# Sums of halves of hT for the second FFN matmul's seven products: two pieces of six inner blocks instead of three of 6, 4 and 2

## The chip, the cores and the metric

The kernel runs on one core of a Trainium2 chip. The core has five engines, each with an instruction queue of its own that is worked off in order: TensorE (PE, with PEld for its weight loads), VectorE (DVE), ScalarE (ACT), GpSimd (POOL) and SyncE (SP), which issues DMAs; POOL issues DMAs too. [...] The metric is device time in microseconds of one execution, and the number quoted is the median of several. Lower is better.

## The reference

Inputs are q, k, v of shape (8, 12, 448, 64) and two FFN weights, 768 x 3072 and 3072 x 768. What is computed:

```python
scores = scale * np.matmul(q, k.transpose(0, 1, 3, 2))
attn = np.maximum(scores, 0.0) ** 2 / S
x = np.matmul(attn, v)            # then heads side by side: (8, 448, 768)
X = np.fft.fft(np.fft.fft(x, axis=1), axis=2)
u = x + np.real(X)
un = (u - mean(u)) / np.sqrt(var(u) + 1e-06)      # over the 768 channels
out = u + np.maximum(un @ w_ch1, 0.0) @ w_ch2
```

## The kernel before

**Stages.** Attention runs by batch and group of four heads: scores on PE (L954), square of the positive part on ACT and DVE (L967, L981, L984), values on PE (L822 and six L827 in a block). The Fourier mix of a batch is a matmul with cosine and sine tables (L1432), a second small one over rows (L1240), and a normalisation on DVE, ACT and POOL. The normalised rows go through DRAM and come back transposed as unT. The FFN then works on groups of token columns: group 0 has 384 tokens, group 1 has 512, group 2 has 384, and the nine groups behind them 256 each. Its hidden layer hT is kept as 24 blocks of 128 hidden channels.

**First FFN matmul.** L1930 makes hT block by block into PSUM (tiles psF), and a relu, on ACT (L1917) or DVE (L1915), puts it into hT. Groups 8 to 11 do it otherwise, two groups at a time ("joints"; there are two): their first matmul is L1762, with sums of weight quarters made by DVE (L1661) and sums of unT (L1705); ACT takes copies out (L1777, L1806) and DVE adds them up (L1782). Of such two groups the first has its hidden layer in hT and the second in tiles hB.

**Second FFN matmul.** Groups 0 to 2 do some of their 128-token halves as plain products (L1958, L1985). Every other pair of halves, L and R, is done by an object of class `Pair` (L2018 on) with seven products instead of eight. There are eleven pairs: one for each of groups 1 to 7, and two in each joint. With the 24 blocks taken as twelve inner blocks of index 0 (even) and twelve of index 1 (odd), four sums are made on DVE:

- s1 = R0 + R1 (L2047), s2 = s1 - L0 (L2049) and R0 := L0 - R0 in place (L2051), all in `early`;
- L1 := L1 - s2 in place (L2059), in `late`.

The products are L2071, twelve matmuls of 128 x 384 each. Chain A does L0 with W11, then s2 with T2, then s1 with T1, then the new L1 with W22, all into one PSUM bank; chain B does the old L1 with W21, and then, into another, the new R0 with T3 and R1 with T4. T1 to T4 are sums of weights, made by DVE at L1526. Behind most products an addition (L1623, DVE) adds the bank to the output tile o, which comes from DRAM with the residual; the next product of the same chain goes on in the same bank, so it has to wait for that addition. While one chain waits, the other chain's product can run.

**Pieces.** The sums are made in pieces of inner blocks, `CH` (L1486). A piece waits for the relus of its own blocks alone. s1 and s2 have a home for the first six inner blocks (tiles s1, s2) and another for the last six (the upper part of the hT tile, `upper`, which is free from group 1's end on). The second group of a joint cuts the pieces once more where hB changes tile, at inner blocks 6, 8 and 10.

**Order.** All instructions of all engines are placed by a scheduler in the kernel (`Streams.run`, L72): each piece of work is a generator that says which engine it needs, how long it will take there by a formula (for these sums `dve2`, elements/1920 + 0.14 us), and what it waits for. The scheduler always takes the one that can start first by its own clock. So a different length or number of instructions at one place moves what comes behind on every engine. A few matmuls more or less of the FFN are put between attention blocks as they become due.

Of the kernel before, what the change touches and what calls it, by code (L numbers as in the profile page):

```python
# [149 lines left out]
def need(eng, dur, deps=(), bufs=(), ok=None):  # L150
    return eng, dur, list(deps), list(bufs), ok
# [18 lines left out]
def dve2(n):  # L170
    return Port(n / 1920 + 0.14)
# [6 lines left out]
def kernel(  # L178
# [34 lines left out]
    KP = 12  # L213
# [1269 lines left out]
    DH = D // 2  # L1483
    WHOLES = [[0, 1, 2], [2, 3], [2]] + [[]] * (NGR - 3)
    PAIRS = [[], [0]] + [[0]] * (NGR - 2)
    CH = [(0, 6), (6, 10), (10, KP)]  # L1486

    def upper(at, count, width):

        flat = hid[0].rearrange("p j n -> p (j n)")  # L1490
        return flat[:, at:at + count * width].rearrange("p (i n) -> p i n", n=width)

    hid, made = [], []
# [239 lines left out]
    def joint(number):  # L1733
# [112 lines left out]
        for i in range(KP):  # L1846
            sch.add(main(i), (5 + 0.1 * i, 5 + 0.1 * i))
        skip = lambda us: None
        plain = [(k, i0, i1) for k, (i0, i1) in enumerate(CH)]
        cut = [(k, max(i0, c0), min(i1, c1)) for k, (i0, i1) in enumerate(CH) for c0, c1, _ in hb  # L1850
               if max(i0, c0) < min(i1, c1)]
# [22 lines left out]
    def ffn(b):  # L1874
# [49 lines left out]
        for j in range(0, JC, JN):  # L1924
# [9 lines left out]
            if j == JC // 2:  # L1934
                ffn_begun[b].t = e
                at = lambda k, i0, i1, cols: h[:, 2 * i0 + k:2 * i1:2, cols]
                pairs = [Pair(b, c, at, ht, add, advance, [(k, *ch) for k, ch in enumerate(CH)], BF) for c in PAIRS[b]]
                for p in pairs:
# [79 lines left out]
    class Pair:  # L2018
# [14 lines left out]
        def early(self):  # L2033

            at, L, R_ = self.at, self.L, self.R
            if not made:
                yield need("DVE", 0.0, [un_left])
                a1 = work.tile([128, 6, 128], BF16, name="s1", tag="un2", bufs=1)
                a2 = work.tile([128, 6, 128], BF16, name="s2", tag="un3", bufs=1)
                at_ = JC * 256 + KP * DH  # L2040
                for a, m in ((a1, upper(at_, 6, 128)), (a2, upper(at_ + 6 * 128, 6, 128))):
                    made.append([a, m[:, 0:4], m[:, 4:6]])
            for x, (k, i0, i1) in enumerate(self.pieces):
                s1, s2 = (self.sums(n, i0, i1) for n in range(2))
                d = dve2((i1 - i0) * 128)
                yield need("DVE", d, self.ht[2 * i0:2 * i1] + self.waits + ([upper_free] if k else []))
                nc.vector.tensor_tensor(s1, at(0, i0, i1, R_), at(1, i0, i1, R_), op=ALU.add)  # L2047
                yield need("DVE", d)
                nc.vector.tensor_tensor(s2, s1, at(0, i0, i1, L), op=ALU.subtract)  # L2049
                e = yield need("DVE", d)  # L2050
                nc.vector.tensor_tensor(at(0, i0, i1, R_), at(0, i0, i1, L), at(0, i0, i1, R_), op=ALU.subtract)  # L2051
                self.r12[x].t = e + LATENCY["DVE"]
# [10 lines left out]
        def sums(self, n, i0, i1):  # L2063

            k = [c0 <= i0 < c1 for c0, c1 in CH].index(True)
            return made[n][k][:, i0 - CH[k][0]:i1 - CH[k][0]]

# [147 lines left out]
```

## Time and profile before

| | us |
|---|---|
| three runs | 569.48, 569.09, 566.94 |
| median | 569.09 |
| span of the profiled execution | 566.4 |
| PE busy | 556.5 |
| DVE busy | 436.2 |
| ACT busy | 318.2 |
| POOL busy | 195.9 |

The span runs from the first to the last instruction of one execution. Its own time is not listed apart from the span: the span lies 0.5 us below the fastest of the three runs and 2.7 us below their median. Busy time is the time in which an engine had an instruction in work; matmuls are pipelined, so for PE the distance from one matmul's start to the next one's says more than its busy time.

### The profile page before, as it was taken

What the parts mean: (1) busy time and instruction counts of PE and PEld (TensorE: products, weight loads), DVE (VectorE), ACT (ScalarE), POOL (GpSimd) and SP (SyncE); (2) the same over time, 40 slices, a digit from 0 to 9 for tenths busy, and PEclk for the clock granted to TensorE, in tenths of its full rate; (3) what the DMA queues carried; (4) which work ended last, traced back from release to release, by engine and by line L of the source; (5) the groups of instructions that cost most, each with busy time, mean ns of one, the idle gap of its engine ahead of it and who ended that gap; (6) DMA issues with size and microseconds to landing.
All of it is one profiled execution on the core that took longest, in us unless ns stands there. A gap on an engine that the chain in (4) does not pass through costs nothing.

```text
span 566.4 us, 11147 instructions
## 1 busy us (share of the span) xinstructions
PE 556.5 (98%) x4171; PEld 350.1 (62%) x4171; DVE 436.2 (77%) x1016; ACT 318.2 (56%) x536; POOL 195.9 (35%) x281
## 2 busy tenths in 40 slices
PE   7999999999999999999999999999999999999997
PEld 4376556544465455556756757767678688668864
DVE  7976564987789978887997896888899957644762
ACT  5978762676745686585786637638515154015400
POOL 8966225523346234462545545222015000000000
PEclk9999999999999999999999999999999999999999
DMA  9999999979959988899899979956425421231012
GB/s 110 180 209 230 215 215 165 217 144 134 181 96 210 215 117 179 164 187 184 174 163 196 198 121 198 164 123 154 115 65 174 124 75 29 71 127 56 1 57 83
DMA packets 152688, 82.41 MB, mean 146 GB/s; under 512 B 118076, under 2 KB 147900, under 8 KB 152636
## 3 DMA queue, kind: packets, MB, share of 16 engines
q0 software_dynamic: 57056, 33.63, 43.0%
q1 hardware_dynamic: 95580, 48.09, 38.1%
q8 instruction: 32, 0.52, 0.4%
q14 instruction: 20, 0.16, 0.1%
HBM read 62.91 MB, written 26.25 MB: 157 GB/s over the span
## 4 chain that ended last, share of the span: by engine, by line
PE 86%; DMA 5%; DVE 4%; ACT 2%; POOL 1%; issue 1%; DVEq 0%; POOLq 0%; ACTq 0%
PE psF L1930 25%; PE psF L2071 20%; PE psS L1762 8%; PE psS L954 7%; PE psS L2071 5%; DMA kn<-in_k_dram 5%; PE psF L827 5%; PE psF L1985 4%; PE psS L1432 2%; PE psF L1762 2%; PE psF L1958 2%; PE psF L822 1%; PE psF L623 1%; DVE sq L984 1%; PE psS L827 1%
## 5 line engine op out<-in xcount | busy, mean ns | idle before, releaser
L1930 PE MATMUL psF<-unT,w 128*128 128x256 bf16 (+2 forms) x1152 | 165.3, 299 | 0.0
L967 ACT ACTIVATE sq<-psS 128x896 bf16<-128x896 f32 x168 | 144.1, 919 | 31.7 <-PE psS L954 31.2
L1930 PEld LDWEIGHTS <-w 128*128 128x128 bf16 x1152 | 110.9, 98 | 49.6 <-issue 5.2
L984 DVE TENSOR_TENSOR sq<-sq 128x896 bf16<-128x896 bf16 x144 | 88.9, 634 | 13.3 <-ACT sq L967 12.5
L2071 PEld LDWEIGHTS <-hT 128*128 128x128 bf16 x648 | 62.5, 98 | 44.1 <-issue 4.8
L1917 ACT ACTIVATE hT<-psF 128x512 bf16<-128x512 f32 (+2 forms) x121 | 59.6, 508 | 41.1 <-PE psF L1930 40.3
L1623 DVE TENSOR_TENSOR o<-psF,o 128x384 f32<-128x384 f32 (+1 forms) x78 | 42.6, 547 | 24.3 <-PE psF L2071 20.8
L2071 PE MATMUL psF<-w,hT 128*128 128x384 bf16 x336 | 59.7, 326 | 0.6 <-DVE o L1623 0.6
L954 PE MATMUL psS<-qkT 64*128 64x448 bf16 (+1 forms) x336 | 51.5, 354 | 1.0 <-DVE qkT L630 0.8
L1777 ACT COPY copies<-psS 128x256 f32<-128x256 f32 x57 | 19.9, 374 | 53.0 <-PE psS L1762 48.1
L689 DVE TENSOR_SCALAR xT<-psF 128x224 bf16<-128x224 f32 x60 | 20.6, 384 | 26.1 <-PE psF L827 26.1
L1275 POOL TENSOR_TENSOR u<-tp,xn 112x385 f32<-112x385 f32 (+2 forms) x14 | 14.5, 1037 | 72.6 <-DVE tp L1255 48.6
L476 POOL DMA_DIRECT2D qn<-in_q_dram x21 | 15.7, 747 | 57.7 <-DVE qkr L583 50.3
L827 PE MATMUL psF<-sq,vn 128*64 128x448 bf16 x246 | 33.0, 362 | 0.0
L954 PEld LDWEIGHTS <-qkT 64*128 64x128 bf16 (+1 forms) x336 | 12.9, 94 | 32.3 <-issue 26.4
L1762 PEld LDWEIGHTS <-w 128*128 128x128 bf16 x288 | 28.2, 98 | 4.7 <-issue 1.1
L451 POOL DMA_DIRECT2D kn<-in_k_dram x42 | 25.9, 626 | 10.3 <-DMA w<-in_moe_w_ch_dram 6.0
L1284 DVE BATCH_NORM_STATS2 stats<-u 112x6 f32<-112x384 f32 (+2 forms) x56 | 28.7, 543 | 0.8 <-POOL u L1275 0.6
L451 POOL DMA_DIRECT2D vn<-in_v_dram x42 | 26.1, 638 | 6.2 <-DMA w<-in_moe_w_ch_dram 5.4
L476 POOL DMA_DIRECT2D vn<-in_v_dram x24 | 18.9, 789 | 25.5 <-PE psS L954 25.4
L1303 ACT ACTIVATE un<-u,small 112x768 bf16<-112x768 f32 (+2 forms) x22 | 22.0, 1023 | 9.5 <-DVE small L1290 8.4
L1782 DVE CUSTOM_DVE_ANT_0 hT<-psS,copies 128x256 bf16<-128x256 f32 x37 | 15.0, 421 | 14.1 <-PE psS L1762 6.2
(238 smaller groups left out, 946.9 us busy)
## 6 DMA issues: line engine op xcount, KB each, us to landing
out_dram<-o SPq DMA_DIRECT2D x55, 192.0 KB, 2.3
qn<-in_q_dram POOLq DMA_DIRECT2D x21, 224.0 KB, 5.1
vn<-in_v_dram POOLq DMA_DIRECT2D x24, 192.0 KB, 5.6
w<-in_moe_w_ch_dram POOLq DMA_DIRECT2D x12, 384.0 KB, 11.8
w<-in_moe_w_ch_dram POOLq DMA_DIRECT2D x4, 1152.0 KB, 23.4
kn<-in_k_dram POOLq DMA_DIRECT2D x21, 192.0 KB, 5.9
utop<-u SPq DMA_DIRECT2D x12, 336.0 KB, 2.9
o<-utop SPq DMA_DIRECT2D x16, 192.0 KB, 3.7
```

What stands on the lines that cost most here:

```text
L451: nc.gpsimd.dma_start(out=t[par * Dh:(par + 1) * Dh, par::2], in_=at)
L476: nc.gpsimd.dma_start(out=to, in_=src[b, hs, 0:rows].rearrange("h (p j) d -> p h (j d)", j=j))
L827: nc.tensor.matmul(av[h * Dh:(h + 1) * Dh, 0:S], lhsT=vn_home[:, at:at + Dh], rhs=sq[:, h, :], start=start, stop=stop, skip_group_check=True)
L954: nc.tensor.matmul(sc[:, h, 0:S].rearrange("k (c q) -> k c q", c=4), lhsT=flat[ps, k0:k0 + KB], rhs=qT[ps, pair], start=True, stop=True)
L967: nc.scalar.activation(r, sc[:, :, 0:S], AF.Relu)
L984: nc.vector.tensor_tensor(r, r, r, op=ALU.mult)
L1284: nc.vector.bn_stats(stats[:n, hf, :], u[:n, hf * (D // 2):(hf + 1) * (D // 2)])
L1623: nc.vector.tensor_tensor(o[:, cols], pc[:, cols], o[:, cols], op=ALU.add)
L1762: nc.tensor.matmul(ps[:, 0:N], lhsT=lhs, rhs=rhs[:, m], start=(start and m == 0), stop=(stop and m == 2), skip_group_check=True)
L1917: nc.scalar.activation(hs, ps, AF.Relu)
L1930: nc.tensor.matmul(ph[:, i * N:(i + 1) * N], lhsT=w1_sb[m][hf][:, (jj + i) * 128:(jj + i + 1) * 128], rhs=unT[:, m, 0:N], start=(m == 0), ...
L2071: nc.tensor.matmul(pc[:, cols], lhsT=lhs[i], rhs=rhs[i][:, cols], start=(start and i == 0), stop=(i == KP - 1), skip_group_check=True)
```

## The change

The table of pieces gets two entries instead of three, and the list of homes for s1 and s2 follows.

```diff
     WHOLES = [[0, 1, 2], [2, 3], [2]] + [[]] * (NGR - 3)
     PAIRS = [[], [0]] + [[0]] * (NGR - 2)
-    CH = [(0, 6), (6, 10), (10, KP)]
+    CH = [(0, 6), (6, KP)]
...
                 for a, m in ((a1, upper(at_, 6, 128)), (a2, upper(at_ + 6 * 128, 6, 128))):
-                    made.append([a, m[:, 0:4], m[:, 4:6]])
+                    made.append([a, m])
             for x, (k, i0, i1) in enumerate(self.pieces):
```

No matmul is added or removed, and none changes its size; PE has 4171 before and behind the change. The scheduler's order is the same up to the first pair of group 1, and another one from there on. Three places show how.

The first is VectorE at the first pair, group 1 (o is the output tile, sq belongs to attention, s_2067 is the tile s2, and hT's upper part holds the last halves of s1 and s2). Before:

```order
L2047 TENSOR_TENSOR hT<-hT 128x512
L2049 TENSOR_TENSOR hT<-hT 128x512
L2051 TENSOR_TENSOR hT<-hT 128x4x128
L1623 TENSOR_TENSOR o<-psF,o 128x384
L984 TENSOR_TENSOR sq<-sq 128x896
L2047 TENSOR_TENSOR hT<-hT 128x256
L2049 TENSOR_TENSOR hT<-hT 128x256
L1623 TENSOR_TENSOR o<-psF,o 128x384
L2051 TENSOR_TENSOR hT<-hT 128x2x128
L2059 TENSOR_TENSOR hT<-hT,s_2067 128x6x128
L2059 TENSOR_TENSOR hT<-hT 128x4x128
```

And of the change, the same place:

```order
L2047 TENSOR_TENSOR hT<-hT 128x768
L2049 TENSOR_TENSOR hT<-hT 128x768
L1623 TENSOR_TENSOR o<-psF,o 128x384
L984 TENSOR_TENSOR sq<-sq 128x896
L2051 TENSOR_TENSOR hT<-hT 128x6x128
L1526 TENSOR_TENSOR hT<-w_0_976,wsum 128x1152
L1623 TENSOR_TENSOR o<-psF,o 128x384
L2059 TENSOR_TENSOR hT<-hT,s_2067 128x6x128
L2059 TENSOR_TENSOR hT<-hT 128x6x128
```

Two instructions of 512 and 256 elements have become one of 768 in each of the four steps, and a weight sum (L1526) has moved ahead of the second addition.

The second place is VectorE at the end of the last joint, where the last sums of hT are made behind the last L1782 (copies and psS are what it adds up; quarter is a home of s1 and s2 of the joint's second group). Before:

```order
L2047 TENSOR_TENSOR hT<-hT 128x512
L2049 TENSOR_TENSOR hT<-hT 128x512
L1782 ISA hB<-psS,copies 128x256
L2051 TENSOR_TENSOR hT<-hT 128x4x128
L2047 TENSOR_TENSOR quarter<-hB 128x256
L2049 TENSOR_TENSOR quarter<-quarter,hB 128x256
L2051 TENSOR_TENSOR hB<-hB 128x2x128
```

and, behind a second such set of three and the last L1782:

```order
L1782 ISA hT<-psS,copies 128x256
L2047 TENSOR_TENSOR hT<-hT 128x256
L2049 TENSOR_TENSOR hT<-hT 128x256
L2051 TENSOR_TENSOR hT<-hT 128x2x128
L1623 TENSOR_TENSOR o<-psF,o 128x384
L2059 TENSOR_TENSOR hT<-hT,s_2067 128x6x128
```

Of the change, the same end:

```order
L1782 ISA hT<-psS,copies 128x256
L2047 TENSOR_TENSOR hT<-hT 128x768
L2049 TENSOR_TENSOR hT<-hT 128x768
L2051 TENSOR_TENSOR hT<-hT 128x6x128
L1623 TENSOR_TENSOR o<-psS,o 128x384
L2059 TENSOR_TENSOR hT<-hT,s_2067 128x6x128
```

The work on the four inner blocks that stood ahead of the last L1782 now stands behind it.

The third place is TensorE behind the last value block of attention (L827). Before, group 6's pair follows at once:

```order
L827 LDWEIGHTS vn
L827 MATMUL psS<-sq,vn 64x448
L2071 LDWEIGHTS hT
L2071 MATMUL psF<-w_3_1061,hT 128x384
L2071 LDWEIGHTS hT
L2071 MATMUL psF<-w_3_1061,hT 128x384
L2071 LDWEIGHTS hT
L2071 MATMUL psF<-w_3_1061,hT 128x384
L2071 LDWEIGHTS s_2067
L2071 MATMUL psF<-wsum,s_2067 128x384
```

Of the change, it is the first FFN matmul of group 6:

```order
L827 LDWEIGHTS vn
L827 MATMUL psF<-sq,vn 64x448
L1930 LDWEIGHTS w_0_1_585
L1930 MATMUL psF<-unT,w_0_1_585 128x256
L1930 LDWEIGHTS w_1_1_608
L1930 MATMUL psF<-unT,w_1_1_608 128x256
L1930 LDWEIGHTS w_2_1_633
L1930 MATMUL psF<-unT,w_2_1_633 128x256
```

From there to the first matmul of the first joint (L1762) stand, before, 144 matmuls of L1930 and 147 of L2071, besides 24 of L1432 and four small ones; of the change, 204 of L1930, 168 of L2071, and the same of the others. So attention ends earlier in TensorE's queue, with more of the FFN behind it. The L1762 of the first joint also stand otherwise: 192 ahead of its first L2071 before, 201 now, which is the arrangement that the second joint has in both kernels.

## The prediction

> **What bounds the kernel now.** I read the page first: busy shares and slices (tenths).
>
> ```profile
> span 566.4 us, 11147 instructions
> PE 556.5 (98%) x4171; PEld 350.1 (62%) x4171; DVE 436.2 (77%) x1016; ACT 318.2 (56%) x536; POOL 195.9 (35%) x281
> PE   7999999999999999999999999999999999999997
> DVE  7976564987789978887997896888899957644762
> ```
>
> TensorE is busy in every slice between the first and the last; VectorE, which the change touches, has idle time in most slices. Busy matmuls overlap, so I then asked what TensorE waited for from 120 us on. The order of the two kernels is the same up to the first pair's second piece (first row: the sums into hT run from 180.5 us on), so the other rows hold all that the change can take away on TensorE.
>
> ```profile
> L2047 DVE TENSOR_TENSOR hT<-hT x18: 239/332/420, 180.5 to 540.6; 128x512 bf16<-128x512 bf16 x9, 128x256 bf16<-128x256 bf16 x9
> ```
>
> ```profile
> PE psF L2071 <- DVE o L1623: 0.9, 2, 0.6
> PE psS L1762 <- DVE hT L1782: 0.5, 2, 0.3
> PE psF L822 <- ACT hT L1917: 0.2, 1, 0.2
> ```
>
> That is 0.9 + 0.5 + 0.2 = **1.6 us of waits in 446 us**. The chain of work that ended last (its time, length, engine and line) shows that there is no slack between matmuls either:
>
> ```profile
> 427.58 10.48 PE psF L1930 x96
> 438.06 13.65 PE psF L2071 x84
> ...
> 506.67 1.31 PE psS L1762 x12
> ```
>
> 96 matmuls of 256 columns take 10.48 us, 0.109 each, and 84 of 384 columns 13.65, 0.1625 each; the ratio of the two is that of their columns. A chain that goes from TensorE to TensorE like this ends no earlier because another engine does less.
>
> [...]
>
> **VectorE's instructions.** Groups by form, with count, busy time and mean ns:
>
> ```profile
> L2059 DVE TENSOR_TENSOR hT<-hT,s 128x768 bf16<-128x768 bf16 x9 | 4.9, 549 | 0.0
> L2059 DVE TENSOR_TENSOR hT<-hT 128x512 bf16<-128x512 bf16 x9 | 3.8, 419 | 0.0
> L2059 DVE TENSOR_TENSOR hT<-hT 128x256 bf16<-128x256 bf16 x9 | 2.6, 284 | 0.0
> ```
>
> Nine pairs have 6, 4 and 2 inner blocks; the two hB pairs are cut at hB's own borders and keep their four pieces, so there the change does nothing. In the nine, four steps lose one instruction each: 36 fewer. By durations, 512 and 256 cost 419 + 284 = 703 ns and 768 costs 549, so 154 ns are saved each, 5.5 us in all. But instructions overlap. The timeline of VectorE (start, length) gives the real spacing:
>
> ```profile
> 469.45 0.55 DVE L2047 TENSOR_TENSOR s<-hT 128x768 bf16<-128x768 bf16 x1
> 470.04 0.56 DVE L2049 TENSOR_TENSOR s<-s,hT 128x768 bf16<-128x768 bf16 x1
> ...
> 474.42 0.55 DVE L2051 TENSOR_TENSOR hB<-hB 128x768 bf16<-128x768 bf16 x1
> 474.89 0.28 DVE L2047 TENSOR_TENSOR ownsum<-hB 128x256 bf16<-128x256 bf16 x1
> ...
> 480.44 0.42 DVE L2049 TENSOR_TENSOR hT<-hT 128x512 bf16<-128x512 bf16 x1
> 480.78 0.42 DVE L2051 TENSOR_TENSOR hT<-hT 128x512 bf16<-128x512 bf16 x1
> ```
>
> 768 takes 0.47 to the next start, 512 takes 0.34, and 256 takes 0.21 (540.91 to 541.12, below). So 0.34 + 0.21 - 0.47 = 0.08 each, **2.9 us** in all, and 5.5 is the upper end. Either is hidden behind TensorE's 98%: I count **0 on the path**.
>
> [...]
>
> **The second piece comes later.** What the small last piece did is shown at the very end, where little covers it. VectorE, then TensorE:
>
> ```profile
> 540.12 0.42 DVE L1782 CUSTOM_DVE_ANT_0 hT<-psS,copies 128x256 bf16<-128x256 f32 x1 [0.45 <-PE psS L1762]
> 540.58 0.29 DVE L2047 TENSOR_TENSOR hT<-hT 128x256 bf16<-128x256 bf16 x1
> 540.91 0.29 DVE L2049 TENSOR_TENSOR hT<-hT 128x256 bf16<-128x256 bf16 x1
> 541.12 0.28 DVE L2051 TENSOR_TENSOR hT<-hT 128x256 bf16<-128x256 bf16 x1
> 542.56 0.56 DVE L1623 TENSOR_TENSOR o<-psF,o 128x384 f32<-128x384 f32 x1 [1.16 <-PE psF L2071]
> ```
>
> ```profile
> 542.85 1.14 PE L2071 MATMUL psS<-wsum,s 128*128 128x384 bf16 x6
> 543.82 3.09 PE L2071 MATMUL psS<-wsum,hT 128*128 128x384 bf16 x18
> ```
>
> Behind the last hidden block the three sums now take 0.82 us (540.58 to 541.40). With 768 elements they take 0.59 (469.45 to 470.04, the second waits for the first) + 0.47 + 0.55 = 1.6 us, so they end at 542.2, **0.8 us later**. s2's last half is read at 543.82 at the earliest, R0 six matmuls behind that, and the addition at 542.56 that stands behind them is not held up. Even from 542.2 that leaves 1.6 us. In groups 1 to 7 the cover is larger: two first products, 24 matmuls of 0.1625 = 3.9 us, lie between the last relu and s2's first reader, in both orders, against relu and 1.6 us of sums. So 0; if that cover were gone in all nine, it would be 9 x 0.8 = 7 us. L2059 is shorter than before, so nothing waits there.
>
> The wait itself is no longer one. The second piece stands at the head of VectorE's queue until the relu of its last block, and additions (L1623) and attention's squares (L984) are queued behind it; the old third piece stood for that same relu. What changes is that the work on four blocks, which could be done ahead of that relu, is now done behind it: the 0.8 us already counted.
>
> **The order behind it.** Matmuls are the same, and so are the counts of places where TensorE goes over from attention to something else and back: 0. What moves is attention. Between its last value block and the first joint stand 60 more L1930 and 21 more L2071: 60 x 0.109 + 21 x 0.1625 = 9.9 us. So attention has to be ready 9.9 us earlier. Is that possible? Windows up to and behind the first pair, L827's own first, then all engines (width; busy us and count of PE, PEld, DVE, ACT, POOL; clock, DMA share, GB/s):
>
> ```profile
> 118.60:196.80 78.20, 7.59 (x60) 2.54 (x60) 1.00 1.03 161
> 196.80:409.00 212.20, 19.38 (x156) 6.60 (x156) 1.00 0.94 164
> ```
>
> ```profile
> 118.60:196.80 78.20, 78.00 (x474) 37.86 (x472) 64.08 (x148) 49.78 (x68) 31.41 (x44) 1.00 1.03 161
> 196.80:409.00 212.20, 211.34 (x1593) 133.68 (x1590) 178.15 (x401) 140.95 (x226) 87.94 (x107) 1.00 0.94 164
> ```
>
> Six L827 are one block. The first stretch did 10 blocks in 78.2 us, 7.8 each, at 82% of VectorE, with TensorE busy for 78.00; the second did 26 in 212.2, 8.2 each. The new order asks for 26 in 202.3, which is 7.8 again, with VectorE at (178 - 3)/202 = 87%. The kernel has held that pace, so I take 0. Its ends: the waits on L1623 (0.9 us) may go, or come several times (second rival).
>
> Of chain handovers that have nothing of the other chain or of attention in between there is one before (s1's product and L1's, group 2) and one now (group 3). It costs what the first row below shows; the second row is a handover of chain B with two score matmuls in it.
>
> ```profile
> 258.85 2.11 PE L2071 MATMUL psF<-w,hT 128*128 128x384 bf16 x12 [0.65 <-DVE o L1623]
> ...
> 296.31 2.11 PE L2071 MATMUL psF<-hT 128*128 128x384 bf16 x12 [0.21 <-DVE o L1623]
> ```
>
> So 0 between them. In the joints, both waits on L1782 are in the second one, which begins at 506.67:
>
> ```profile
> 514.83 0.81 PE L1762 MATMUL psS<-sumx,w 128*128 128x256 bf16 x6 [0.30 <-DVE hT L1782]
> ...
> 536.02 0.49 PE L1762 MATMUL psS<-chan,w 128*128 128x256 bf16 x3 [0.19 <-DVE hT L1782]
> ```
>
> The first joint now has the second one's arrangement of matmuls, so I let it pay the same: **+0.5 us**. Bounds: 0, and twice that.
>
> **Sum.** 0 (matmuls) + 0 (VectorE, hidden) + 0 (late piece) + 0 (attention's pace) + 0.5 (first joint) = 566.4 + 0.5 = 566.9 us of span. The median of the runs lies 2.7 above the span before, and nothing in the change bears on that: **569.6 us**.
>
> **Rivals.**
>
> *VectorE's gain goes through.* If VectorE set the pace after all, 2.9 to 5.5 us would go: 563.6 to 566.2. For it: VectorE is at 90% or more in ten of the forty slices. Against it: TensorE waited for VectorE for 1.4 us only, so the span's own ceiling is 569.1 - 1.6 = 567.5. [...] Chance 0.08.
>
> *Handovers wait behind a denser VectorE queue (slower).* A chain's next product needs its L1623. VectorE works in order; if more than 1.95 - 0.56 = 1.4 us of other work (three of the long sums) stand ahead of the addition when its product ends, the other chain's twelve matmuls no longer cover it and TensorE stands, 0.65 us as in the row above. The eleven pairs have three handovers each, 33; two waited before. VectorE's rise from 84% to 87% and single instructions of 768 elements speak for it, fewer instructions against it. It decides from about six waits on: 6 x 0.65 - 0.9 = +3.0, 572.1 us; ten give +5.6, 574.7. Chance 0.29, since the new order has not been seen and each of its waits can only cost.
>
> *The change does less than it says* is true for the two hB pairs and in the sum already.
>
> **How the numbers follow.** Forecast 0.63, slower rival 0.29, VectorE's gain 0.08. A measurement of this kernel can tell about 0.5%, 2.8 us, from no change: 566.2 to 571.9 counts as the same. The forecast lies inside, the second rival nearly all above, the first nearly all below. Chances: faster 0.08, same 0.63, slower 0.29. The forecast's own range is 567.5 to 571.9; the range of 8 in 10 goes up to 574.0, into the slower rival, and down to 567.0.
>
> **What would show it.** TensorE's busy time within 1 us of 556.5; VectorE's 3 to 6 us lower; TensorE's waits behind 120 us at about 2 us; the first joint waiting on L1782 for 0.3 to 0.5; the last value block near 399 us; s2's last half done before its reader in the last joint. I am wrong if TensorE waits on L1623 at many handovers, if it waits for qkT or sq in the denser attention, or if the chain of waits runs through VectorE.

## The result, and the profile after

| | before | after |
|---|---|---|
| runs, us | 566.94 to 569.48 (5) | 570.52, 570.77, 571.50, 573.90, 574.73 |
| median, us | 568.16 | 571.50 |
| ratio, 95% interval | | 1.0073 [1.0049, 1.0097] |
| span of the profiled execution, us | 566.4 | 568.7 |

The changed kernel is 0.73% slower by the ratio on record, which is taken over the runs of both kernels and not from the two medians (their quotient is 1.0059). Its profiled execution took 570.52 us, 1.8 more than its span. The page of after, with its busy times and the slices of PE:

```profile
span 568.7 us, 11103 instructions
PE 557.9 (98%) x4171; PEld 350.1 (62%) x4171; DVE 431.0 (76%) x981; ACT 322.7 (57%) x537; POOL 194.8 (34%) x279
PE   8999999999999999989999999999999999999997
```

VectorE has 5.2 us less to do, as meant, and PE 1.4 us more; slice 18 of PE (counted from 1) is no longer full. What PE waited for from 120 us on (total, times, longest):

```profile
PE psF L2071 <- DVE xT L689: 1.5, 1, 1.5
PE psF L2071 <- DVE o L1623: 0.6, 1, 0.6
PE psS L1762 <- DVE hT L1782: 0.6, 2, 0.3
PE psS L1762 <- ACT copies L1777: 0.4, 2, 0.2
PE psS L2071 <- DVE hT L1782: 0.3, 1, 0.3
PE psS L1762 <- DVE o L1623: 0.2, 1, 0.2
PE psS L954 <- DMA qkT<-qkr: 0.2, 1, 0.2
...
```

Before it was 1.6 us in all; the rows here already hold 3.8. The largest is new and is a single wait of 1.5 us. Those in the joints (L1762, and L2071 behind L1782) have grown from 0.5 to 1.5.

To see how much each part of the program lost I cut the span at three matmuls that both kernels have: the first product of the first pair, the first matmul of the first joint, and the last product. The views by line give their starts (min, median and max ns of one; first and last start in us). Before:

```profile
L2071 PE MATMUL psF<-w,hT x336: 322/326/337, 179.3 to 542.2; 128*128 128x384 bf16 x168
L1762 PE MATMUL psS<-unT,w x114: 272/273/273, 451.5 to 528.0; 128*128 128x256 bf16 x114
L2071 PE MATMUL psF<-w,hB x60: 246/326/326, 478.7 to 562.3; 128*128 128x384 bf16 x36, 128*128 128x192 bf16 x24
```

After:

```profile
L2071 PE MATMUL psF<-w,hT x294: 322/326/336, 178.3 to 452.3; 128*128 128x384 bf16 x147
L1762 PE MATMUL psS<-unT,w x108: 272/273/273, 452.5 to 530.9; 128*128 128x256 bf16 x108
L2071 PE MATMUL psF<-w,hB x60: 246/326/326, 485.9 to 564.6; 128*128 128x384 bf16 x36, 128*128 128x192 bf16 x24
```

The first stretch, in which nothing was changed, was 1.0 us shorter in this execution (178.3 against 179.3; before has a wait of 1.0 us for ACT there, at L1205, that the other lacks). From there to the joints, "the groups" below, it is 452.5 - 178.3 = 274.2 against 451.5 - 179.3 = 272.2: **2.0 us lost**. The joints take 564.6 - 452.5 = 112.1 against 562.3 - 451.5 = 110.8: **1.3 us lost**. So 3.3 in all, which is also the difference of the medians.

What holds PE up near 244 us is told by the chain of waits of after (start, length, engine and line):

```profile
232.97 1.24 POOL u L1277
...
234.22 1.19 SPq L796
...
238.31 4.16 DMA qkT<-qkr
...
242.59 0.56 DVE qkr L583
243.15 0.86 DVE fold L770 x2
244.01 0.60 DVE xT L689 x2
...
244.66 3.59 PE psF L2071 x21
```

Read from below: the pair's product needs a PSUM bank that L689 empties; L689 stands behind two folds, and those behind a copy of attention's next keys (L583), which waits until the transpose of the keys before them has read its buffer. That transpose stood on SyncE's queue behind three transposes into xn (L796, the first of them shown), which in turn waited for POOL. In the kernel before, SyncE issued that transpose ahead of those into xn:

```profile
236.05 1.28 SPq L593 DMA_TRANSPOSE qkT<-qkr  x1
...
240.36 5.43 SPq L796 DMA_TRANSPOSE xn<-xT  x4
```

No instruction of the changed sums is in the chain. Two readings were open: that the larger, later pieces cost the time, or that the order, drawn up anew by the scheduler around them, does.

### The profile page after: what moved, and what is told of

Read it like the earlier page. It is cut to its first block, busy times and chain, and to the rows that moved or that the text cites. A ratio compares the mean times of both kernels' runs of the same rounds, so it can differ in the third digit from the quotient of the medians.

```text
span 568.7 us, 11103 instructions
## 1 busy us (share of the span) xinstructions
PE 557.9 (98%) x4171; PEld 350.1 (62%) x4171; DVE 431.0 (76%) x981; ACT 322.7 (57%) x537; POOL 194.8 (34%) x279
## 4 chain that ended last, share of the span: by engine, by line
PE 87%; DVE 3%; POOL 2%; DMA 2%; ACT 2%; issue 1%; SPq 1%; DVEq 0%; POOLq 0%; ACTq 0%
PE psF L1930 24%; PE psF L2071 20%; PE psS L954 7%; PE psS L2071 7%; PE psS L1762 7%; PE psF L827 4%; PE psF L1958 4%; PE psF L1985 3%; PE psS L1432 2%; PE psF L1762 2%; DMA qkT<-qkr 2%; PE psF L822 1%; PE psS L827 1%; PE psF L623 1%; SPq L796 1%
## 5 line engine op out<-in xcount | busy, mean ns | idle before, releaser
L1930 PE MATMUL psF<-unT,w 128*128 128x256 bf16 (+2 forms) x1152 | 165.6, 299 | 0.2
L1930 PEld LDWEIGHTS <-w 128*128 128x128 bf16 x1152 | 110.8, 98 | 50.0 <-issue 6.0
L984 DVE TENSOR_TENSOR sq<-sq 128x896 bf16<-128x896 bf16 x141 | 85.3, 620 | 14.3 <-ACT sq L967 13.6
L2071 PEld LDWEIGHTS <-hT 128*128 128x128 bf16 x648 | 62.5, 98 | 46.2 <-issue 4.7
L2071 PE MATMUL psF<-w,hT 128*128 128x384 bf16 x294 | 52.1, 326 | 2.2 <-DVE xT L689 1.5
L1623 DVE TENSOR_TENSOR o<-psF,o 128x384 f32<-128x384 f32 (+1 forms) x73 | 39.7, 545 | 16.9 <-PE psF L2071 14.3
L1777 ACT COPY copies<-psS 128x256 f32<-128x256 f32 x48 | 17.3, 375 | 55.9 <-PE psS L1762 28.1
L689 DVE TENSOR_SCALAR xT<-psF 128x224 bf16<-128x224 f32 x56 | 19.2, 384 | 25.1 <-PE psF L827 25.1
L1275 POOL TENSOR_TENSOR u<-tp,xn 112x385 f32<-112x385 f32 (+2 forms) x14 | 13.9, 994 | 70.8 <-DVE tp L1255 43.5
L827 PE MATMUL psF<-sq,vn 128*64 128x448 bf16 x234 | 31.5, 363 | 0.0
L1762 PEld LDWEIGHTS <-w 128*128 128x128 bf16 x288 | 28.2, 98 | 4.4 <-issue 0.4
L1303 ACT ACTIVATE un<-u,small 112x768 bf16<-112x768 f32 (+2 forms) x24 | 23.9, 1022 | 9.6 <-DVE small L1290 9.6
L1782 DVE CUSTOM_DVE_ANT_0 hT<-psS,copies 128x256 bf16<-128x256 f32 x40 | 16.3, 421 | 13.9 <-ACT copies L1777 5.8
```

What stands on the lines that cost most here:

```text
L827: nc.tensor.matmul(av[h * Dh:(h + 1) * Dh, 0:S], lhsT=vn_home[:, at:at + Dh], rhs=sq[:, h, :], start=start, stop=stop, skip_group_check=True)
L984: nc.vector.tensor_tensor(r, r, r, op=ALU.mult)
L1623: nc.vector.tensor_tensor(o[:, cols], pc[:, cols], o[:, cols], op=ALU.add)
L1762: nc.tensor.matmul(ps[:, 0:N], lhsT=lhs, rhs=rhs[:, m], start=(start and m == 0), stop=(stop and m == 2), skip_group_check=True)
L1930: nc.tensor.matmul(ph[:, i * N:(i + 1) * N], lhsT=w1_sb[m][hf][:, (jj + i) * 128:(jj + i + 1) * 128], rhs=unT[:, m, 0:N], start=(m == 0), ...
L2071: nc.tensor.matmul(pc[:, cols], lhsT=lhs[i], rhs=rhs[i][:, cols], start=(start and i == 0), stop=(i == KP - 1), skip_group_check=True)
```

## The experiments

Ratios are to the kernel before on the same chip (its median was 567.53 us beside e1 to e4, 567.74 beside e5 to e8 and 568.01 beside e9 to e12). Each ratio is the one on record; it is not the quotient of the two medians, from which it differs by up to 0.14%. The last columns are the stretches from above, from the same matmuls of each profile; they were worked out before rounding, so a last digit can be one off the rounded rows.

| run | median, us | ratio, 95% interval | groups | joints |
|---|---|---|---|---|
| before | | | 272.2 | 110.8 |
| after | 571.50 | 1.0073 [1.0049, 1.0097] | 274.2 | 112.1 |
| e1 order of before, two pieces | 568.23 | 1.0013 [0.9998, 1.0028] | 272.9 | 110.7 |
| e2 order of after, three pieces | 572.25 | 1.0078 [1.0058, 1.0097] | 277.0 | 112.1 |
| e3 two pieces in the groups | 572.94 | 1.0086 [1.0066, 1.0106] | 276.8 | 112.1 |
| e4 two pieces in the joints | 567.95 | 1.0007 [0.9998, 1.0015] | 272.2 | 110.9 |
| e5 after, one copy later | 569.56 | 1.0036 [1.0022, 1.0049] | 273.3 | 112.1 |
| e6 after, one transpose first | 569.90 | 1.0037 [1.0023, 1.0050] | 273.3 | 112.1 |
| e7 before, redrawn | 575.47 | 1.0123 [1.0105, 1.0141] | 278.3 | 112.4 |
| e8 before, redrawn otherwise | 573.66 | 1.0108 [1.0092, 1.0123] | 275.5 | 112.4 |
| e9 after, two transposes first | 568.89 | 1.0014 [1.0002, 1.0025] | 272.4 | 112.1 |
| e10 pause, short | 571.83 | 1.0067 [1.0048, 1.0085] | 275.2 | 112.1 |
| e11 pause, long | 575.60 | 1.0137 [1.0115, 1.0158] | 278.2 | 112.3 |
| e12 before, joints redrawn | 570.47 | 1.0048 [1.0030, 1.0066] | 272.2 | 113.0 |

**e1 and e2: the instructions and the order apart.** In e1 the scheduler books three pieces as before, but the second piece's instructions are left out and the third's made to cover both:

```diff
+                j0 = 6 if (i0, i1) == (10, KP) and len(self.pieces) == 3 else i0
+                held = (i0, i1) == (6, 10)
+                s1, s2 = (self.sums(n, j0, i1) for n in range(2))
                 yield need("DVE", d, self.ht[2 * i0:2 * i1] + self.waits + ([upper_free] if k else []))
-                nc.vector.tensor_tensor(s1, at(0, i0, i1, R_), at(1, i0, i1, R_), op=ALU.add)
+                if not held:
+                    nc.vector.tensor_tensor(s1, at(0, j0, i1, R_), at(1, j0, i1, R_), op=ALU.add)
...
```

> Every engine's instructions stand as in the kernel before, except that the middle piece (4 inner blocks) and the third (2 blocks) of the sums are issued as one instruction of 6 blocks at the third piece's place, so VectorE has 36 instructions fewer. Theory 1 (the larger, later second piece costs the time: it stands longer in VectorE's queue and its readers wait): 571 to 572 us, about 3.3 over the kernel before, as the change itself. Theory 2 (the instructions cost nothing; the schedule that was drawn up anew around them costs): 567.5 to 568.5 us, the kernel before's time within 0.2%, with VectorE's busy time 3 to 6 us lower and PE's waits from 120 us at 1.5 to 2 us. Theory 3 (the difference between the two kernels is the chip's spread and no property of either): this kernel and the next differ by less than 1 us.

In e2 the scheduler books two pieces, and each instruction of the second is issued as two:

```diff
+                parts = [(6, 10), (10, KP)] if (i0, i1) == (6, KP) else [(i0, i1)]
                 yield need("DVE", d, self.ht[2 * i0:2 * i1] + self.waits + ([upper_free] if k else []))
-                nc.vector.tensor_tensor(s1, at(0, i0, i1, R_), at(1, i0, i1, R_), op=ALU.add)
+                for j0, j1 in parts:
+                    nc.vector.tensor_tensor(self.sums(0, j0, j1), at(0, j0, j1, R_), at(1, j0, j1, R_), op=ALU.add)
...
```

> The mirror of the run before: every engine's instructions stand as in the changed kernel, but each instruction of the second piece is issued as two, of 4 and of 2 blocks, one behind the other, so VectorE has the kernel before's number of instructions. Theory 1: 568 to 569 us, the kernel before's time. Theory 2: 571 to 572.5 us, 0.5 to 0.8% over the kernel before, with PE waiting 3 to 5 us from 120 us on, among it over 1 us for the first product of the second group's pair behind xT L689 near 244 us. Theory 3: within 1 us of the run before.

e1 has the pieces of after and the time of before; e2 has the pieces of before and the time of after. Theory 3 falls, and so does theory 1 as an account of the 3.3 us. The busy times of e1's page, where before had 436.2 us of VectorE:

```profile
PE 557.6 (98%) x4171; PEld 350.1 (62%) x4171; DVE 434.2 (77%) x980; ACT 318.6 (56%) x536; POOL 196.2 (35%) x281
```

And e2's, where after had 431.0:

```profile
PE 558.9 (98%) x4171; PEld 350.3 (61%) x4171; DVE 432.7 (76%) x1017; ACT 322.6 (56%) x537; POOL 193.3 (34%) x279
```

So 36 instructions fewer save 2.0 us of VectorE in the one order and 1.7 in the other, and the span nothing: e1 had been expected at 3 to 6 us less. PE's waits in e1 are 1.8 us, as expected of theory 2, but one of them is not in the kernel before, and it does go back to the merged sums:

```profile
286.28 1.27 DVE L2056 TENSOR_TENSOR hT<-hT 128x768 bf16<-128x768 bf16 x1
```

```profile
288.68 1.64 PE L2078 MATMUL psF<-w,hT 128*128 128x384 bf16 x9 [0.54 <-DVE xT L689]
```

The first row is the last of three merged sums, which stand behind the relu of their last block; L1275 and then L689 stand behind them on VectorE, and PE waits for L689, which begins 1.1 us later than before. The row is also 0.7 us longer than the 0.56 us of the two sums ahead of it; an instruction of POOL (L1275) runs beside it, from 286.19 us on, and in before the last sum had ended at 286.25. Whether the one lengthened the other is not shown. These 0.7 us are more than the wait. So theory 1 is left with one wait of 0.54 us, and one profile doesn't say whether every execution has it; e1's groups are 0.7 us longer than before's. In e2 the wait near 244 us was 2.4 us instead of 1.5.

**e3 and e4: where.** Two pieces in the groups alone (from after: `CH` again has three pieces, which the joints use, and the groups' pairs are built from `CH2 = [(0, 6), (6, KP)]`):

```diff
-                pairs = [Pair(b, c, at, ht, add, advance, [(k, *ch) for k, ch in enumerate(CH)], BF) for c in PAIRS[b]]
+                pairs = [Pair(b, c, at, ht, add, advance, [(k, *ch) for k, ch in enumerate(CH2)], BF) for c in PAIRS[b]]
```

> Two pieces in the groups of the first and middle part alone; the two joints at the end keep three pieces. TensorE, ScalarE, POOL and SP stand as in the changed kernel, VectorE differs in the joints alone. Theory 2 puts about 2.3 us of the loss in the groups (the wait of 1.5 us near 244 us and smaller ones) and about 1 us in the joints: 570 to 571 us. If the joints make nearly all of it: 568 to 569. Theory 1 gives the same ratio as the number of pairs, nine tenths of the loss: 571 us.

And in the joints alone (again with three pieces in `CH`, which the groups use here, so that they stand as in before):

```diff
-        plain = [(k, i0, i1) for k, (i0, i1) in enumerate(CH)]
-        cut = [(k, max(i0, c0), min(i1, c1)) for k, (i0, i1) in enumerate(CH) for c0, c1, _ in hb
+        plain = [(k, i0, i1) for k, (i0, i1) in enumerate(CH2)]
+        cut = [(k, max(i0, c0), min(i1, c1)) for k, (i0, i1) in enumerate(CH2) for c0, c1, _ in hb
```

> Two pieces in the joints alone; everything ahead of the first joint stands as in the kernel before. Theory 2 with the loss mainly in the groups: 568.5 to 569.5 us, at most 1 us over the kernel before, PE's waits in the joints about 1.5 us against 0.5. If the joints make nearly all of the loss: 571 to 572 us.

e3 loses all of it, more than the 570 to 571 us I gave it, and that includes 1.3 us in joints that still have three pieces. e4 loses nothing that can be told, although its joints do have two. What the joints lose in the changed kernel therefore isn't made by their pieces either. What is left is their order of matmuls and banks, which depends on the state in which the scheduler's clock comes to them; e12 below tests that an order alone can do it.

e3 also shows something of the spread. The order of after gives times in two groups: e2 has four executions up to 572.53 us at a mean clock of 0.999 or more and two above 574 at 0.996, e3 three up to 571.83 and three above 574 at 0.997 or less. e3's profile is one of the long ones. Its matmuls behind the wait:

```profile
247.58 5.27 PE L2072 MATMUL psF<-w,hT 128*128 128x384 bf16 x21 [2.40 <-DVE xT L689]
```

In after the same 21 took 3.59 us (last row of the chain above). The windows of e3 from 246 us on (width; busy us and count of PE, PEld, DVE, ACT, POOL; granted clock, DMA share, GB/s):

```profile
246.00:248.00 2.00, 0.42 (x3) 0.30 (x4) 2.00 (x7) 1.25 (x2) 1.64 (x3) 1.00 1.20 331
248.00:250.00 2.00, 2.00 (x9) 1.01 (x8) 1.72 (x4) 0.00 (x0) 0.34 (x1) 0.55 1.32 179
250.00:252.00 2.00, 2.00 (x9) 0.96 (x8) 0.94 (x3) 0.00 (x0) 0.00 (x0) 0.59 1.84 182
252.00:254.00 2.00, 2.00 (x17) 0.76 (x14) 1.06 (x3) 0.00 (x0) 0.00 (x0) 1.00 1.23 105
```

Behind a wait of 2.4 us the granted clock was 0.55 to 0.59 for some 4 us, which cost 5.27 - 3.59 = 1.7 us more. In the profile of after the wait was 1.5 us and the clock stayed at 1.00. So one place costs 1.5 us in one execution and 4.1 in another; the copy waits 2.00 us in after, 2.94 in e2 and 2.99 in e3 for that transpose, whose landing the chains of waits give as 4.16, 5.34 and 5.21 us.

**e5 and e6: the one wait.** e5 is after with the copy issued behind L689 on VectorE, the only instruction that moves:

```diff
-                    nc.vector.tensor_copy(o, loads[b * NG + g][x])
+                    copied[0] += x
+                    if x and copied[0] == 11:
+                        late.append((o, loads[b * NG + g][x]))
+                    else:
+                        nc.vector.tensor_copy(o, loads[b * NG + g][x])
...
+                if en == "DVE" and late:
+                    nc.vector.tensor_copy(*late.pop())
```

> The changed kernel with one VectorE instruction moved: the copy of kn into qkr that waits 2 us for a transpose near 242 us is issued behind the two folds L770 and the two evictions L689 instead of ahead of them; nothing else stands elsewhere on any engine. Theory 2a (the loss in the groups is this one wait and the lowered clock that follows it, the loss in the joints is 1.4 us from their order): PE's wait on xT L689 near 244 us goes from 1.5 to 2.4 us to under 0.3, no stretch between 246 and 254 us has a granted clock under 0.95, no execution takes over 572 us unless its clock falls elsewhere, and the median is 569 to 570 us, 0.25 to 0.45% over the kernel before. Theory 2b (the wait is only the place where a delay shows that the whole order has, denser queues that lose the time at another place): the wait comes back within 20 us at another row and the median stays at 571 us or more.

e6 is after with the transpose of the keys ahead of the three into xn on SyncE, again with nothing else moved (the three are kept back until it has been issued):

```diff
+                    if x and copied[0] == 10:
+                        copied[1] = True
...
-        nc.sync.dma_start_transpose(out=xns[b][:, :, m * 128:(m + 1) * 128], in_=xTc[m])
+        if copied[1]:
+            late.append((xns[b][:, :, m * 128:(m + 1) * 128], xTc[m]))
+        else:
+            nc.sync.dma_start_transpose(out=xns[b][:, :, m * 128:(m + 1) * 128], in_=xTc[m])
```

> The changed kernel with one SyncE instruction moved: the transpose of the second half of qkr into qkT near 238 us is issued ahead of the three transposes of xT into xn (L796) that start near 234 us, as in the kernel before, instead of behind them. Theory 2a, with the cause on SyncE's queue: the copy of kn no longer waits for that transpose, the wait on xT L689 near 244 us is under 0.3, and the median is as in the run before, 569 to 570 us. If the order of SyncE's queue isn't the cause (the transposes are slow for another reason): the copy waits on as before and the median is 571 to 572.5 us.

Both take away half of the loss, to 569.56 and 569.90 us, none of their executions is above 570.84, and their clocks stay at 0.999 or more. The cause of this wait is the order on SyncE's queue, and either end of the chain undoes it. PE's waits in e6, though, show that a part came back at another place:

```profile
PE psS L966 <- DMA qkT<-qkr: 1.0, 1, 1.0
```

The scores at 313 us now wait 1.0 us for qkT (0.2 in after): PE comes there earlier, and the transpose doesn't. Theories 2a and 2b were each right by half.

**e9: both places.** On SyncE's queue in after (the timeline: start, length) that transpose stands behind one into unT:

```profile
302.45 3.98 SPq L1380 DMA_TRANSPOSE unT<-ntop  x1
...
307.10 2.55 SPq L593 DMA_TRANSPOSE qkT<-qkr  x1
```

In before the same transpose stood ahead of it:

```profile
305.56 1.70 SPq L593 DMA_TRANSPOSE qkT<-qkr  x1
...
308.22 2.48 SPq L1380 DMA_TRANSPOSE unT<-ntop  x1
```

e9 is e6 with the same exchange there. Its edit does one thing more: at the first place, too, a transpose into unT is now kept back, so that the keys' transpose (at 232.48 us) stands ahead of that one (233.99) as well as of the three into xn:

```diff
-                    if x and copied[0] == 10:
+                    if x and copied[0] in (10, 14):
...
-                nc.sync.dma_start_transpose(out=g[:, :, t - GT[k]:t - GT[k] + w], in_=src[r0:r0 + w, :])
+                if copied[1]:
+                    late.append((g[:, :, t - GT[k]:t - GT[k] + w], src[r0:r0 + w, :]))
+                else:
+                    nc.sync.dma_start_transpose(out=g[:, :, t - GT[k]:t - GT[k] + w], in_=src[r0:r0 + w, :])
```

> The changed kernel with SyncE's order mended at two places: the transpose of the second half of qkr into qkT goes ahead of the three transposes into xn near 234 us, and the one near 307 us ahead of the transpose into unT. The run with the first place alone got rid of the wait near 244 us, but PE then waited 1.0 us for qkT near 312 us (0.2 in the changed kernel). If that second wait also is a matter of the place on SyncE's queue, it goes under 0.3 and the median falls by a further 0.6 to 0.8 us, to 568.8 to 569.3 us; what is left over the kernel before is the 1.4 us of the joints. If the transposes are late for their own sake, the wait stays near 1 us and the median at 569.5 to 570.

568.89 us, 1.0014, as expected. Of PE's waits only those of the joints and the known handover are left over 0.3 us:

```profile
PE psF L2087 <- DVE o L1639: 0.6, 1, 0.6
PE psS L1778 <- DVE hT L1798: 0.6, 2, 0.3
PE psS L1778 <- ACT copies L1793: 0.4, 2, 0.2
```

The groups take 272.4 us, what they took before, with attention as dense as in after. So these two places on SyncE's queue make the whole loss of the groups; how much of it, if any, the further transpose at the first place gave is not told apart. The joints' 112.1 are still there.

**e7 and e8: the same instructions, drawn up anew.** The kernel before, with another cost booked for each of the sums of `early`, -0.01 us in e7 and +0.03 in e8:

```diff
-                d = dve2((i1 - i0) * 128)
+                d = Port(dve2((i1 - i0) * 128) - 0.01)
```

> The kernel before, three pieces, with the same instructions; only the cost that the scheduler books for each of the sums is 0.01 us lower, so that it draws up another order (about a thousand instructions stand elsewhere). Theory 2 in its general form (a schedule drawn up anew falls better or worse by some tenths of a per cent whatever caused it, the kernel before being a good draw): 568.5 to 573 us, over the kernel before. If a new draw by itself costs nothing and this change's order is bad because of its pieces: 567 to 568.5 us.

> As the run before, with the booked cost 0.03 us higher instead of 0.01 lower: a second draw with the same instructions. General form of theory 2: 568.5 to 573 us and not the same time as the run before. Otherwise: 567 to 568.5 us.

They lose 1.2% and 1.1%, more than the change did, and more than the upper end I gave. The rows that hold most of it, in e7:

```profile
PE psS L954 <- DMA qkT<-qkr: 4.6, 2, 2.7
```

and in e8:

```profile
PE psF L2071 <- DVE o L1623: 2.6, 2, 2.0
```

Each draw has its own one or two bad places, in e7 again for transposes of keys. The kernel before has none: its draw is better than the three others seen here (after's, e7's and e8's), which is too few to say how rare such a draw is.

**e10 and e11: what a pause of PE costs.** e5 with the second fold at that place written five or eight times more, so that L689 and PE behind it come later:

```diff
-            nc.vector.tensor_tensor(Y[:, w], low, high, op=op)
+            for _ in range(6 if late and w else 1):
+                nc.vector.tensor_tensor(Y[:, w], low, high, op=op)
```

> The kernel of the run with the copy issued later, in which PE didn't wait near 244 us, with one of the folds L770 ahead of the evictions L689 issued five times more (the same result written again): 5 x 0.47 us = 2.35 us of VectorE, of which about 0.8 us is slack, so PE waits about 1.5 us there. Theory on the two groups of times of the changed kernel (a wait of over some 2 us lowers the granted clock for about 4 us behind it, a shorter one doesn't): no granted clock under 0.95 behind the wait, and 570 to 571 us (1.5 us of wait less what the wait for qkT near 312 us gives back). If any wait lowers the clock: 572 us or more.

> As the run before with eight more folds: 3.76 us of VectorE, a wait of about 2.9 us on PE. By the theory the granted clock falls to 0.5 to 0.7 for about 4 us behind it, which costs 1.5 to 2 us on top of the wait: 573 to 574 us, every execution with a mean clock of 0.997 or less. If the wait alone counts: 571.4 to 572 us, 1.4 us over the run before, with the clock at 1.0.

PE behind the pause in e10, with the window there:

```profile
245.27 3.59 PE L2080 MATMUL psF<-w,hT 128*128 128x384 bf16 x21 [1.80 <-DVE xT L695]
```

```profile
246.00:248.00 2.00, 2.00 (x14) 1.21 (x13) 2.00 (x5) 0.00 (x0) 1.82 (x3) 1.00 1.19 213
```

And in e11:

```profile
247.04 5.18 PE L2080 MATMUL psF<-w,hT 128*128 128x384 bf16 x21 [3.48 <-DVE xT L695]
```

```profile
246.00:248.00 2.00, 0.96 (x4) 0.46 (x5) 2.00 (x6) 0.00 (x0) 0.39 (x1) 0.72 1.06 173
248.00:250.00 2.00, 2.00 (x8) 0.99 (x7) 1.51 (x3) 0.00 (x0) 1.59 (x3) 0.50 0.79 100
250.00:252.00 2.00, 2.00 (x13) 1.17 (x12) 1.21 (x4) 0.00 (x0) 0.00 (x0) 0.92 1.46 229
```

The waits were longer than worked out, 1.80 and 3.48 us, since a fold written over itself takes 0.56 us and not 0.47 (the seven folds in a row of e10 take 3.77 us, the ten of e11 5.45). Three folds more lengthen the wait by 1.7 us and the median by 575.60 - 571.83 = 3.8; the 21 matmuls behind it take 5.18 - 3.59 = 1.6 us longer at the lowered clock (0.50 to 0.92 in the windows above). All five executions of e11 have a mean clock of 0.997 or less, all six of e10 one of 0.999 or more. e10 came out 0.8 us over its range and e11 1.6; the longer waits make 0.3 and 0.6 of that, and where the rest comes from stays open.

**e12: the joints alone, drawn up anew.** The kernel before with another booked time in the joints:

```diff
-        d, SLACK, to_go = 3 * mm(N), 0.4, [3 * KP]
+        d, SLACK, to_go = 3 * mm(N), 0.42, [3 * KP]
```

> The kernel before, three pieces; in the two joints alone the scheduler books 0.42 us instead of 0.40 behind each eviction, so that the joints' order is drawn up anew, with everything ahead of the first joint where it stood. If the joints' 1.4 us in the changed kernel is the luck of their order (theory 2): 568.5 to 569.5 us, PE's waits in the joints over 0.8 us against 0.5, by other rows than in the changed kernel or the same. If the joints of the changed kernel are slower because attention ends a block earlier ahead of them: the kernel before's time, 567.5 to 568 us.

The median, 570.47 us, lies 1 us above what was expected. The groups take 272.2 us as before, the joints 113.0 instead of 110.8: 2.2 us, more than in the changed kernel and, for the largest part that a row shows, by another row,

```profile
PE psS L1762 <- DVE o L1623: 0.8, 1, 0.8
```

with attention ahead of them where it was. So the order of the joints alone can cost this much. The rows of waits in the joints add up to 1.5 us in e12 as in after, against 0.5 before, so 1.2 of e12's 2.2 us and 0.3 of after's 1.3 stand in no row. Which exchange would mend the 1.3 us of after's joints was not tried, and none of these versions is faster than the kernel before.

## Why the prediction was right, and where it was wrong

The forecast was 569.6 us and no change that can be told; 571.50 came, inside the range, and slower by over 0.5%, for which it had 0.29. That it lies inside is in part luck: the range was drawn around 569.09, the median of three runs. The median of five is 568.16 and the medians beside the experiments are 567.53 to 568.01; the same 0.5% above 568.16 ends at 571.0. The mechanism of the forecast, that nothing is lost but 0.5 us in the first joint, did not hold. The span forecast was 566.9, and 568.7 came, though the unchanged start was 1.0 us luckier. Of its signs, VectorE's busy time (5.2 us lower) and the place of the last value block came; TensorE's busy time (1.4 us up, not within 1) and its waits (4.0 us in all, not about 2) did not.

- **Matmuls, 0: right.** 4171 as before.
- **VectorE's gain, 2.9 to 5.5 us and hidden: right in kind, too large in size.** It is 1.7 to 2.0 by e1 and e2, below both bounds, and e1 gains nothing from it. The 5.2 us of the page would have seemed to confirm the upper end; more than half of that comes with the other order.
- **The late piece, 0: right for the changed kernel, but not for the reason given.** The forecast looked at the readers of the sums; in e1 it was an eviction behind the sums on VectorE that made PE wait, 0.54 us in one place. e1 as a whole costs 0.13% at an interval that reaches 0. In the order of after even the longest such wait did no harm: VectorE stood 3.80 us for a relu, and no row of PE's waits answers to it.

```profile
439.68 0.56 DVE L2047 TENSOR_TENSOR hT<-hT 128x768 bf16<-128x768 bf16 x1 [3.80 <-ACT hT L1917]
```

- **Attention's pace, 0: right for what it said, and too little.** The last value block did start near 399 us, and e9 shows that PE can be fed in time at that density. But a pace is a mean over 202 us. **This is the step that failed:** "The order behind it" looked at where TensorE goes over from one kind of work to another and at the pace, not at what the new order does on SyncE's queue. There two transposes of keys had slid behind transposes for other work, and the groups lost 2.0 us in the profiled execution (and, at a clock of 0.53 to 0.62 behind the wait, 4.8 in e2's). The text did name a wait for qkT as a sign that it would be wrong; it gave that no price.
- **The first joint, +0.5: the sign was right, the size and the place not.** The joints lost 1.3 us, and all but 0.2 us of the waits there lie in the second one, from 508 us on (the timeline of PE in after):

```profile
510.89 0.49 PE L1762 MATMUL psS<-chan,quarter 128*128 128x256 bf16 x3 [0.29 <-DVE hT L1782]
...
531.82 1.62 PE L2071 MATMUL psS<-w,hT 128*128 128x384 bf16 x9 [0.29 <-DVE hT L1782]
```

I had taken the first joint's arrangement to be the only one that moved.
- **The slower rival** had the wrong place: handovers that wait for L1623 came to one, as forecast, and not to six. Its reason, that each wait of a new order can only cost, was the right one, and by e7 and e8 it deserved more than 0.29.
- **VectorE's gain goes through** (0.08): it did not. e1 has 2.0 us less of VectorE's busy time and the time of before, at a ratio of 1.0013.

## What to carry to other kernels

In a kernel whose order a scheduler draws up, every edit is two changes: what it does, and a new draw. Part them, by holding the order and changing the instructions and the other way round, before either is given the credit or the blame; and draw the unchanged kernel anew once or twice to see how far the draw alone moves the time (here by 0.5 to 1.2%, against 0.13% at an interval that reaches 0 for the edit). Where an order changes, go through every queue, those of the DMAs too, for something that has slid behind work that waits for another engine: one exchange on such a queue was worth as much here as half of the loss.

## What the runs showed of the chip

Some pauses of TensorE cost more here than their own length. Behind waits of 1.52 us (after), 1.80 (e10), 1.87 (e7) and 1.98 (e8) the granted clock stayed at 1.00; behind waits of 2.37 (e2), 2.40 (e3), 2.73 (e7) and 3.48 us (e11) it fell, in the lowest window behind each, to between 0.50 and 0.66, and was back at 1.00 in the window that begins 3.5 us (e2), 4.4 (e3), 6.1 (e7) or 5.0 (e11) behind the end of the wait; the 21 matmuls that took 3.59 us in after took 5.27 in e3 and 5.18 in e11, 1.7 and 1.6 more. The rows of the two waits in e7:

```profile
311.03 0.36 PE L954 MATMUL psS<-qkT 64*128 64x448 bf16 x2 [1.87 <-DMA qkT<-qkr]
355.86 1.30 PE L954 MATMUL psS<-qkT 64*128 64x448 bf16 x6 [2.73 <-DMA qkT<-qkr]
```

and its windows around the second:

```profile
354.00:358.00 4.00, 2.15 (x11) 0.96 (x12) 2.03 (x6) 1.55 (x2) 1.34 (x2) 0.66 1.13 284
358.00:362.00 4.00, 4.00 (x32) 2.80 (x31) 3.04 (x7) 2.88 (x6) 2.60 (x5) 0.91 1.22 136
362.00:366.00 4.00, 4.00 (x39) 3.58 (x38) 4.00 (x7) 3.22 (x6) 0.00 (x0) 1.00 1.39 220
```

Whether the length of the wait alone decides, and where between 1.98 and 2.37 us, stays open. So do one execution of the changed kernel, 573.90 us at a mean clock of 1.00, and one of e1, 571.93 us at 0.996, of which there is no profile.
